# Retention and a SiLU MLP on one core: another order of the engines' work and of the loads from unit 3 to unit 9

## The chip, the cores and the metric

One Trainium2 chip, one of its cores. The metric is the device time of one launch in microseconds; the kernel is judged by the median of its runs. The engines that matter here are TensorE (PE), VectorE (DVE), ScalarE (ACT), GpSimd (POOL) and SyncE (SP), which issues the loads and stores. Each engine works through its own queue in program order; semaphores order the queues against each other.

## The reference

```python
# q, k, v: (B=4, H=8, S=768, D=64)
gamma = 1.0 - 2.0 ** (-5.0 - np.arange(H))
for t in range(S):
    state = gamma[None, :, None, None] * state + np.einsum('bhd,bhe->bhde', k[:, :, t], v[:, :, t])
    y[:, :, t] = scale * np.einsum('bhd,bhde->bhe', q[:, :, t], state)
...
x = y.transpose(0, 2, 1, 3).reshape(B * S, H * D)      # 3072 x 512
h = x @ w_in                                           # w_in: 512 x 2048
g = h * (1.0 / (1.0 + np.exp(-h)))
return g @ w_out                                       # w_out: 2048 x 512
```

A linear attention with a decay for each head, and a two-layer network with SiLU behind it. The weights come as float64 and are converted on the chip.

## The kernel before

**Tiling.** The 768 positions are cut into six chunks of 128. A unit is one chunk of one batch: unit n is chunk n // 4 of batch n % 4, 24 in all. Four units of one chunk make the 512 columns of one block `xt[c]`. The hidden layer has 16 slices of 128 features; a product (c, f) multiplies block c with slice f of w_in, goes through SiLU, and its result g is kept or stored. After all 96 products the output layer runs over the stored g. Each float32 operand is split into a rounded high part and a remainder, so a product has 12 matmuls of 512 columns: i = 0 and i = 1 (four each) sum up in `ha`, i = 2 in `hb`, and the three parts of x and of w are needed in that order.

**One unit.** Its steps have these names in the hand-written order of the first 60 us:

- T(n), `stage_t`: four transposes of k (tile `kp`) and four of q (`qp`) on PE (L482), each followed by a copy on ACT to `kt` and `qt` (L483). `kp` takes one of three PSUM banks in turn, `qp` has one bank.
- K(n), `scale_k`: k times its decay, one DVE instruction in place (L424). KA(n) does the same with eight small ACT instructions, one for each head (L932).
- SC(n): `stage_s`, 32 small matmuls that sum k times v (L510, needs the scaled k), and `stage_a`, 32 for the scores (L520). Both write the bank pair `s`, which is free when unit n-1 has been read out.
- A(n), three steps: DVE masks the scores (`am`, L528); `mid` (L534 on ACT in chunk 0, L536 on DVE later); DVE makes the next `state` (L540).
- Q(n), `scale_q`: q times its decay on DVE (L429), by `gq`, which `next_chunk` moves on by one chunk with four ACT instructions (L379).
- Y(n), `stage_y`: the masked scores times v (32 matmuls), the first half of the states times q, a fence through a one-element POOL memset (L406), and the second half (all L568), in the bank pair `y`. YA(n) is the first two, YB(n) the last.
- X(n), four steps: copy of y to SBUF on ACT (L615), rounding to the high part on ACT (`xh`, L639), the remainder on DVE ("lower", L642), and the third part on DVE ("third", L645).

**Beside the units.** W(i) is one slice of w_in in eleven steps, which convert it from float64 and split it (ACT L205, L212, L121, L127; DVE L208, L214, L218, L224, L124, L129). P(n) is product n (L740, c = n // 16, f = n % 16); `ha` and `hb` take two of the same three banks that `kp` uses, in turn. CL(n) closes it in three steps: copy of `ha` on ACT (L763), subtraction of `hb` on DVE (L768), SiLU on ACT (L773). Some filler matmuls with zeros (L317, L323) stand where PE would wait (`FILL_T` ahead of the transposes, `FILL_FENCE` inside Y, `FILL_P` ahead of a product).

**What sets the order.** PE's order is written out by hand throughout. SP, DVE, ACT and POOL follow the written order up to `early_order.close()`, just behind P(16); from there on a planner sets the order by its own costs and due times, with some places fixed by `issue_after`. Loads are written into SP's order by `load` and `load_w`; loads of units 8 and later rotate through three buffers for k, three for v and two for q; `hold(masked[0])` makes SP wait for the last mask before it goes on.

Of the kernel before, what the change touches and what calls it, by code (L numbers as in the profile page):

```python
# [34 lines left out]
def kernel(  # L35
# [35 lines left out]
    NF = DF // 128  # L71
# [69 lines left out]
    EARLY = 2 * B  # L141
# [32 lines left out]
    def load_w(i):  # L174
        if i >= 2 * NF:
            return
        if wide:
            t = stage.tile([128, 2 * DM], U32, tag="wf", name=f"wf_{i}")
            w_in, w_out, n = moe_w_in.bitcast(U32), moe_w_out.bitcast(U32), 256
        else:  # L180
            t = stage.tile([128, DM], FP32, tag="wf", name=f"wf_{i}")
            w_in, w_out, n = moe_w_in, moe_w_out, 128
        if i < NF:
            to = t.rearrange("p (i o f) -> o p i f", o=2, f=n)
            src = w_in[:, ts(i, n)].rearrange("(i o p) f -> o p i f", o=2, p=128)
            last[:] = [nc.sync.dma_start(out=to[0], in_=src[0]).ins]  # L186
            for j in range(2):
                nc.sync.dma_start(out=to[1, ts(j, D)], in_=src[1, ts(1 - j, D)])  # L188
        else:
            nc.sync.dma_start(out=t, in_=w_out[ts(i - NF, 128), :])  # L190
        staged[i] = t
# [128 lines left out]
    def narrow(out, n):  # L320

        for _ in range(n):
            nc.tensor.matmul(out[:, :32], lhsT=zero, rhs=zero[:, :32], start=True, stop=True,  # L323
                             skip_group_check=True)
# [52 lines left out]
    def next_chunk():  # L377
        for a in range(HP):
            nc.scalar.activation(out=gq[:, a, :], in_=gq[:, a, :], func=AF.Copy,  # L379
                                 scale=step[:, a : a + 1])  # L380
# [75 lines left out]
        nc.scalar.copy(out=to[n].bitcast(U16).rearrange("p a (t w) -> p w a t", w=2),  # L456
                       in_=turned.pop((name, n)).rearrange("p (w a) t -> p w a t", w=2))

    FILL_T = {2: (3, 2), 3: (0, 1)}
    NARROW_T = {0: (8, 5)}  # L460
    FILL_Y = {0: 1, 3: 4}
    NARROW_Y = {0: 8}
    idle = []
    FILL_FENCE = {0: 2, 2: 2, 3: 2}
    FILL_P = {(0, 0): 1, (1, 0): 2}

    def stage_t(n):

        src = kqv["k"][n], kqv["q"].pop(n)
        tp = turn(f"kp_{n}"), banks("q", f"qp_{n}", 1)[:, 0]  # L470

        def new(name, to, bufs):
            to[n] = one.tile([128, HP, C], FP32, tag=name, name=f"{name}_{n}", bufs=bufs)
            return to[n]

        made = ("kt", kt, 2), ("qt", qt, 3)
        if n not in ROWS:
            for i in range(2):
                fill(tp[i], FILL_T.get(n, (0, 0))[i])
                t = tp[i].rearrange("p (a t) -> p a t", a=HP)  # L480
                for a in range(HP):
                    nc.tensor.transpose(t[:, a, :], src[i][:, 2 * a : 2 * a + 2, :], ident)  # L482
                evac[:] = [nc.scalar.copy(out=new(*made[i]), in_=t).ins]  # L483
                if n in NARROW_T:
                    narrow(idle[0], NARROW_T[n][i])
            return
        tp = [t.rearrange("p (i a t) -> p i a t", i=2, a=HP) for t in tp]
        for i in range(2):
            for a in range(HP):
                for o in range(2):  # L490
                    nc.tensor.transpose(tp[o][:, i, a, :], src[i][ts(o, D), 2 * a : 2 * a + 2, :],  # L491
                                        ident[ts(o, D), ts(o, D)])
        made = [new(*m) for m in made]
        for o in range(2):
            for i in range(2):
                evac[:] = [nc.scalar.copy(out=made[i][:, :, ts(o, D)], in_=tp[o][:, i]).ins]
# [52 lines left out]
    def stage_y(n):  # L549

        vs, amn, qtn = kqv["v"].pop(n), am.pop(n), qt.pop(n)
        states = steps_of.pop(n)
        bank = banks("y", f"y_{n}")
        fill(bank[:, 0], FILL_Y.get(n, 0))
        narrow(bank[:, 0], NARROW_Y.get(n, 0))
        yp = bank[:, :, : 4 * D].rearrange("p o (a t) -> p o a t", a=HP)
        lone = None
        if n == len(units) - 1:
            lone = banks("s", f"yl_{n}")[:, :, : 4 * D].rearrange("p o (a t) -> p o a t", a=HP)

        started, done, new = set(), [], []

        def product(a, o, j, lhsT, rhs, apart_now=False):
            e = j ^ (a % 2)
            to = lone if apart_now else yp
            o = o ^ 1 if apart_now else o
            key = apart_now, e, o
            i = nc.tensor.matmul(to[ts(e, D), o, a, :], lhsT=lhsT, rhs=rhs,  # L568
                                 start=key not in started, stop=True,
                                 skip_group_check=True).ins  # L570
            started.add(key)
            if new:
                fence(done[-1], i)
                new.clear()
            done.append(i)

        def scores():
            for a in range(HP):
                for o in range(2):
                    for j in range(2):  # L580
                        product(a, o, j, vs[ts(o, D), 2 * a + j, :], amn[ts(o, D), j, a, :])

# [306 lines left out]
    YA(0), YB(0), X(0)  # L889
    T(1), K(1)  # L890
    W(0)
    load_w(2)
    W(0)
    X(0), X(0)
    SC(1), A(1)
# [8 lines left out]
    YB(1), X(1)  # L904
    A(2), Q(2), A(2)
    X(1)
    T(3), K(3)
    X(1), X(1)
    YA(2), YB(2), X(2)
    SC(3), A(3), A(3), Q(3), A(3)  # L910
    X(2), W(1), W(1)
    X(2), X(2)
    YA(3), YB(3), X(3), X(3)
    W(1), W(1)
    T(4)
    X(3), X(3)
    K(4)
    W(1), W(1)
    loads(EARLY - 2), loads(EARLY - 1)
    closing = {}  # L920

    def P(n):
        c, f = divmod(n, NF)
        closing[n] = close_steps(c, f, *multiply(c, f))

    def CL(f):
        next(closing[f], None)

    def KA(n):
        t = kqv["k"][n]  # L930
        for h in range(H):
            nc.scalar.activation(out=t[:, h, :], in_=t[:, h, :], func=AF.Copy,  # L932
                                 scale=gk[:, units[n][0], h : h + 1])

    P(0)
    next_chunk()
    SC(4)
    CL(0), CL(0), CL(0)
    put_g(0)
    W(1)  # L940
    T(5)
    A(4), A(4), Q(4), K(5), A(4)
    W(1), W(1)
    YA(4), SC(5), YB(4)
    loads(EARLY)
    W(2), W(1)
    A(5)
    W(1), W(2), W(2)
    X(4)
    T(6)  # L950
    P(1)
    A(5), Q(5), A(5)
    KA(6)
    W(2), W(2), W(2)
    load("k", EARLY + 1), load("q", EARLY + 1), load("v", EARLY + 1)
    W(2)
    CL(1), CL(1)
    W(2)
    YA(5), SC(6), YB(5)
    X(5)  # L960
    W(2), W(2)
    A(6)
    W(2)
    CL(1)
    put_g(0)
    T(7)
    P(2)
    K(7), A(6), Q(6), A(6)
    X(4), X(5), X(4), X(4)
    CL(2)  # L970
    YA(6), SC(7), YB(6)
    X(6)
    T(8)
    A(7)
    hold(masked[0])
    load("k", EARLY + 2), load("q", EARLY + 2)
    load_w(3)
    load("v", EARLY + 2)
    load_w(4)
    A(7), Q(7)  # L980
    next_chunk()
    K(8), A(7)
    CL(2), CL(2)
    put_g(0)
    X(5), X(5)
    X(6)
    YA(7), SC(8), YB(7)
    X(7), X(7)
    A(8)
    X(6), X(6)  # L990
    T(9)
    load("k", EARLY + 3), load("q", EARLY + 3)
    X(7), X(7)
    A(8), Q(8), A(8)
    P(NF)
    KA(9)
    CL(NF), CL(NF)
    taken[0] = 3
    begin_w()
    CL(NF)  # L1000
# [194 lines left out]
```

## Time and profile before

| | |
|---|---|
| runs | 611.75, 612.47, 614.08 us, median 612.47 |
| profiled execution | 611.64 us, span 609.5 us |
| granted TensorE clock | 1.00 throughout |
| HBM traffic | 66.06 MB read, 36.70 MB written |
| written order ends (end of P(16)) | about 55.2 us into the span |

The span runs from the first to the last instruction of the profile. Views of the trace used in this document: busy time by stretches, timelines of one engine, the waits (who waited for whom), and the loads with their time to landing. Times in them are from the start of the span; an end of a matmul is modelled, the starts are recorded. Behind 56 us PE runs without a wait that the view of waits names.

### The profile page before, as it was taken

The numbers are of one execution on the slowest core, as the hardware profiler recorded it, in microseconds if no ns is written. First come the engines' busy times: TensorE is split into PE (matmuls) and PEld (weight loads), VectorE is DVE, ScalarE is ACT, GpSimd is POOL, SyncE is SP. The second block draws the span as 40 slices with busy tenths as digits, with TensorE's granted clock in tenths as the row PEclk, the third lists the DMA queues.
The fourth block names the chain that finished last, engine by engine and source line by source line (L and its number), as shares of the span: only waits on it lengthen the run. The fifth ranks groups of instructions, "written<-read, shape, count | busy, mean of one in ns | idle before, by whom it ended". The sixth has DMA issues, their size and how long they took to land.

```text
span 609.5 us, 13714 instructions
## 1 busy us (share of the span) xinstructions
PE 600.8 (99%) x5509; PEld 495.8 (81%) x5509; DVE 396.3 (65%) x673; ACT 325.0 (53%) x599; POOL 33.3 (5%) x89
## 2 busy tenths in 40 slices
PE   8999999999999999999999999999999999999997
PEld 6787788888888888888888888888888888888886
DVE  4888998678876766766699765535454553645532
ACT  7788777678776677666789622221221412313111
POOL 3000110100031112110000000000000000000000
PEclk9999999999999999999999999999999999999999
DMA  9998787776799699999777433524423342533201
GB/s 195 215 213 194 190 224 250 238 238 203 252 246 209 173 271 270 246 265 283 258 266 239 157 122 100 176 69 127 151 100 109 138 129 79 171 105 112 96 1 69
DMA packets 144335, 108.90 MB, mean 179 GB/s; under 512 B 101136, under 2 KB 109584, under 8 KB 144272
## 3 DMA queue, kind: packets, MB, share of 16 engines
q1 hardware_dynamic: 144272, 108.03, 62.7%
q8 instruction: 43, 0.70, 0.5%
q14 instruction: 20, 0.16, 0.1%
HBM read 66.06 MB, written 36.70 MB: 169 GB/s over the span
## 4 chain that ended last, share of the span: by engine, by line
PE 93%; SPq 4%; DVE 2%; DMA 1%; ACT 0%; issue 0%; DVEq 0%
PE ha L740 29%; PE o L1117 21%; PE hb L740 14%; PE oa L1117 14%; PE ob L1117 7%; PE y L568 3%; SPq L166 3%; PE sc L510 1%; PE sc L520 1%; DMA kqv<-in_q_dram 1%; PE o L1137 0%; SPq L188 0%; PE kp L482 0%; SPq L186 0%; PE kp L491 0%
## 5 line engine op out<-in xcount | busy, mean ns | idle before, releaser
L740 PE MATMUL ha<-xt,wi 128*128 128x512 f32 x768 | 193.0, 393 | 0.4 <-DVE xt L642 0.3
L740 PEld LDWEIGHTS ha<-xt,wi 128*128 128x128 f32 x768 | 142.4, 188 | 31.4 <-DVE xt L642 0.8
L1117 PE MATMUL o<-wo,gs 128*128 128x512 f32 x564 | 143.1, 389 | 0.0
L828 ACT ACTIVATE gs<-gr 128x512 fp32r<-128x512 f32 x96 | 53.2, 621 | 139.0 <-issue 138.0
L1117 PEld LDWEIGHTS o<-wo,gs 128*128 128x128 f32 x564 | 105.9, 188 | 22.0
L830 DVE TENSOR_TENSOR gs<-gr,gs 128x512 fp32r<-128x512 f32 x96 | 62.1, 684 | 94.2 <-ACT gs L828 94.2
L1117 PE MATMUL oa<-wo,gs 128*128 128x512 f32 x376 | 115.7, 389 | 0.0
L740 PE MATMUL hb<-xt,wi 128*128 128x512 f32 x384 | 102.6, 389 | 0.0
L768 DVE TENSOR_TENSOR g<-g,hb 128x512 f32<-128x512 f32 x87 | 59.5, 684 | 53.8 <-ACT g L763 41.2
L740 PEld LDWEIGHTS hb<-xt,wi 128*128 128x128 f32 x384 | 72.1, 188 | 15.1
L1117 PEld LDWEIGHTS oa<-wo,gs 128*128 128x128 f32 x376 | 70.5, 188 | 14.6
L1117 PE MATMUL ob<-wo,gs 128*128 128x512 f32 x188 | 73.1, 389 | 0.0
L773 ACT ACTIVATE g<-g 128x512 f32<-128x512 f32 x87 | 54.7, 628 | 33.3 <-DVE g L768 33.1
L763 ACT ACTIVATE g<-ha 128x512 f32<-128x512 f32 x87 | 51.7, 594 | 27.0 <-PE ha L740 18.1
L831 DVE SCALAR_TENSOR_TENSOR gs<-gs 128x512 fp32r<-128x512 f32 x96 | 62.0, 683 | 0.1
L1117 PEld LDWEIGHTS ob<-wo,gs 128*128 128x128 f32 x188 | 35.3, 188 | 7.3
L205 ACT ACTIVATE ca<-wf 128x512 f32<-128x512 f32 x32 | 21.6, 674 | 7.2 <-DVE cs L218 3.1
L1158 ACT ACTIVATE o<-o 128x512 f32<-128x512 f32 x10 | 6.0, 600 | 33.4 <-PE o L1117 33.0
L218 DVE SCALAR_TENSOR_TENSOR cs<-ca,cs 128x512 uint32<-128x512 uint32 x32 | 23.2, 725 | 0.9
L528 DVE TENSOR_TENSOR am<-sc,decay 128x512 f32<-128x512 f32 x24 | 16.5, 688 | 10.3 <-PE sc L520 10.2
L645 DVE SCALAR_TENSOR_TENSOR xt<-xt 128x512 fp32r<-128x512 f32 x28 | 20.1, 724 | 0.7
L568 PE MATMUL y<-qt,mid 64*64 64x64 f32 x376 | 19.4, 219 | 0.3 <-issue 0.3
(132 smaller groups left out, 580.6 us busy)
## 6 DMA issues: line engine op xcount, KB each, us to landing
gr<-gd SPq DMA_DIRECT2D x96, 256.0 KB, 2.7
gd<-g SPq DMA_DIRECT2D x87, 256.0 KB, 3.5
wf<-in_moe_w_out_dram SPq DMA_DIRECT2D x16, 512.0 KB, 4.8
out_dram<-o SPq DMA_DIRECT2D x23, 256.0 KB, 2.1
wf<-in_moe_w_in_dram SPq DMA_DIRECT2D x16, 256.0 KB, 4.1
wf<-in_moe_w_in_dram SPq DMA_DIRECT2D x32, 128.0 KB, 4.1
kf<-in_k_dram SPq DMA_DIRECT2D x16, 256.0 KB, 4.5
qf<-in_q_dram SPq DMA_DIRECT2D x16, 256.0 KB, 4.3
```

Of the source, the lines that this page charges most:

```text
L205: top = nc.scalar.activation(out=a.bitcast(FP32), in_=hi.bitcast(FP32), func=AF.Abs, scale=2.0 ** -3).ins
L218: nc.vector.scalar_tensor_tensor(out=s, in0=a, scalar=3, in1=s, op0=ALU.logical_shift_left, op1=ALU.bitwise_xor)
L568: i = nc.tensor.matmul(to[ts(e, D), o, a, :], lhsT=lhsT, rhs=rhs, start=key not in started, stop=True, skip_group_check=True).ins
L645: nc.vector.scalar_tensor_tensor(out=x[2], in0=x[1].bitcast(FP32), scalar=-1.0 / EPS, in1=x[0].bitcast(FP32), op0=ALU.mult, op1=ALU.add)
L740: nc.tensor.matmul(hb if i == 2 else ha, lhsT=w_sb[f][:, i, ts(kk, 128)], rhs=xt[c][:, i, kk, :], start=kk == 0 and i != 1, stop=kk == KIN ...
L763: copied[:] = [nc.scalar.activation(out=hs, in_=ha, func=AF.Copy, scale=ONE_E).ins]
L768: taken_out[:] = [nc.vector.tensor_tensor(out=hs, in0=hs, in1=hb, op=ALU.subtract).ins]
L773: nc.scalar.activation(out=hs, in_=hs, func=AF.Silu)
L828: nc.scalar.activation(out=t[:, 0, :], in_=g, func=AF.Copy, scale=HALF)
L830: nc.vector.tensor_tensor(out=t[:, 1, :], in0=g, in1=high, op=ALU.subtract)
L831: nc.vector.scalar_tensor_tensor(out=t[:, 2, :], in0=t[:, 1, :].bitcast(FP32), scalar=-1.0 / EPS, in1=high, op0=ALU.mult, op1=ALU.add)
L1117: nc.tensor.matmul(o, lhsT=g, rhs=wo[f][:, i, :], start=f == 0 and i != 1, stop=f == NF - 1 and i != 0 or (b, f, i) == (B - 1, early_f - 1 ...
```

## The change

The part of the written order from T(3) to P(16) is replaced by another one, with the same steps. Single pieces that differ: T(n) and YA(n) can be called in halves (TK and TQ, YS and Y0), so that a unit's k and q transposes can stand apart; two fillers are taken out (`FILL_T` of unit 3, `FILL_FENCE` of unit 2); unit 7's k is scaled by KA on ACT and not by K on DVE; both halves of Y(7) stand ahead of SC(8) on PE; the k half of T(6) stands ahead of SC(5), and the q half behind YB(4); CL(0) stands behind both halves of T(5); `next_chunk` stands ahead of unit 3's copy of y and, the second time, ahead of CL(2)'s SiLU. On SP, the third slice of w_in goes out behind unit 6's q, unit 9's v ahead of unit 8's, and unit 10's k and the fourth slice ahead of the hold. The products are each issued whole, as before.

```diff
-    FILL_T = {2: (3, 2), 3: (0, 1)}
+    FILL_T = {2: (3, 2)}
...
-    FILL_FENCE = {0: 2, 2: 2, 3: 2}
+    FILL_FENCE = {0: 2, 3: 2}
...
     def stage_t(n):
+        list(steps_t(n))
+
+    def steps_t(n):
...
                 if n in NARROW_T:
                     narrow(idle[0], NARROW_T[n][i])
+                yield
             return
...
+    tsteps = {}
+
+    def TK(n):
+        tsteps[n] = steps_t(n)
+        next(tsteps[n])
+
+    def TQ(n):
+        next(tsteps[n])
+
     def YA(n):
+        YS(n), Y0(n)
+
+    def YS(n):
         ys[n] = stage_y(n)
         ys[n][0]()
+
+    def Y0(n):
         ys[n][1](0)
...
-    load_w(2)
...
-    T(3), K(3)
-    X(1), X(1)
-    YA(2), YB(2), X(2)
-    SC(3), A(3), A(3), Q(3), A(3)
-    X(2), W(1), W(1)
-    X(2), X(2)
-    YA(3), YB(3), X(3), X(3)
-    W(1), W(1)
-    T(4)
-    X(3), X(3)
-    K(4)
-    W(1), W(1)
-    loads(EARLY - 2), loads(EARLY - 1)
...
-    P(0)
-    next_chunk()
-    SC(4)
-    CL(0), CL(0), CL(0)
-    put_g(0)
-    W(1)
-    T(5)
-    A(4), A(4), Q(4), K(5), A(4)
-    W(1), W(1)
-    YA(4), SC(5), YB(4)
-    loads(EARLY)
-    W(2), W(1)
-    A(5)
-    W(1), W(2), W(2)
-    X(4)
-    T(6)
-    P(1)
-    A(5), Q(5), A(5)
-    KA(6)
-    W(2), W(2), W(2)
-    load("k", EARLY + 1), load("q", EARLY + 1), load("v", EARLY + 1)
-    W(2)
-    CL(1), CL(1)
-    W(2)
-    YA(5), SC(6), YB(5)
-    X(5)
-    W(2), W(2)
-    A(6)
-    W(2)
-    CL(1)
-    put_g(0)
-    T(7)
-    P(2)
-    K(7), A(6), Q(6), A(6)
-    X(4), X(5), X(4), X(4)
-    CL(2)
-    YA(6), SC(7), YB(6)
-    X(6)
-    T(8)
-    A(7)
-    hold(masked[0])
-    load("k", EARLY + 2), load("q", EARLY + 2)
-    load_w(3)
-    load("v", EARLY + 2)
-    load_w(4)
-    A(7), Q(7)
-    next_chunk()
-    K(8), A(7)
-    CL(2), CL(2)
-    put_g(0)
-    X(5), X(5)
-    X(6)
-    YA(7), SC(8), YB(7)
-    X(7), X(7)
-    A(8)
-    X(6), X(6)
-    T(9)
-    load("k", EARLY + 3), load("q", EARLY + 3)
-    X(7), X(7)
-    A(8), Q(8), A(8)
-    P(NF)
-    KA(9)
-    CL(NF), CL(NF)
```

In the diff above the old order stands whole. The new order, which the full diff has one call to a line, here with several to a line and nothing left out:

```python
TK(3) X(1) load("k",6) YS(2) TQ(3) Y0(2) K(3) X(1) YB(2) X(2) X(2) SC(3) A(3) A(3) W(1) Q(3)
load("q",6) load_w(2) YS(3) X(2) load("k",7) next_chunk() A(3) Y0(3) YB(3) W(1) X(3) X(3)
load("v",6) TK(4) load("q",7) TQ(4) X(2) W(1) load("v",7) W(1) W(1) W(1) X(3) X(3)
load("v",9) K(4) W(1) P(0) SC(4) A(4) A(4) W(1) Q(4) TK(5) A(4) TQ(5) K(5) load("q",8)
YS(4) CL(0) W(1) Y0(4) TK(6) SC(5) CL(0) YB(4) W(1) Q(5) CL(0) X(4) A(5) W(1) W(2) W(2)
load("k",8) A(5) A(5) TQ(6) W(2) KA(6) W(2) P(1) load("q",9) load("k",9) W(2) W(2)
YS(5) CL(1) Y0(5) put_g(0) SC(6) W(2) CL(1) Q(6) load("v",8) W(2) W(2) A(6) YB(5) X(4)
W(2) A(6) X(5) load_w(3) W(2) TK(7) TQ(7) CL(1) X(4) A(6) P(2) load("k",10) KA(7) X(4)
YS(6) CL(2) X(5) Y0(6) put_g(0) SC(7) YB(6) X(6) CL(2) TK(8) TQ(8) A(7) Q(7) A(7) YS(7)
K(8) Y0(7) next_chunk() X(5) CL(2) YB(7) hold(masked[0]) A(7) X(7) X(5) X(6) X(6) X(7)
TK(9) SC(8) X(7) load("v",10) load_w(4) load("q",10) A(8) load("k",11) TQ(9) put_g(0)
A(8) X(7) KA(9) X(6) P(NF) load("q",11) Q(8) CL(NF) A(8) CL(NF)
```

More of the change, by code (lines that the diff above doesn't have):

```diff
@@ L933, in KA @@
                                  scale=gk[:, units[n][0], h : h + 1])
+    TK(3)
+    X(1)
+    load("k",6)
+    YS(2)
+    TQ(3)
+    Y0(2)
+    K(3)
+    X(1)
+    YB(2)
+    X(2)
+    X(2)
+    SC(3)
+    A(3)
+    A(3)
+    W(1)
+    Q(3)
+    load("q",6)
+    load_w(2)
+    YS(3)
+    X(2)
+    load("k",7)
+    next_chunk()
+    A(3)
+    Y0(3)
+    YB(3)
+    W(1)
+    X(3)
+    X(3)
+    load("v",6)
+    TK(4)
+    load("q",7)
+    TQ(4)
+    X(2)
+    W(1)
+    load("v",7)
+    W(1)
+    W(1)
@@ L935 @@
+    W(1)
+    X(3)
+    X(3)
+    load("v",9)
+    K(4)
+    W(1)
     P(0)
-    next_chunk()
     SC(4)
-    CL(0), CL(0), CL(0)
-    put_g(0)
-    W(1)
-    T(5)
-    A(4), A(4), Q(4), K(5), A(4)
-    W(1), W(1)
-    YA(4), SC(5), YB(4)
-    loads(EARLY)
-    W(2), W(1)
-    A(5)
-    W(1), W(2), W(2)
-    X(4)
-    T(6)
-    P(1)
-    A(5), Q(5), A(5)
-    KA(6)
-    W(2), W(2), W(2)
-    load("k", EARLY + 1), load("q", EARLY + 1), load("v", EARLY + 1)
-    W(2)
-    CL(1), CL(1)
-    W(2)
-    YA(5), SC(6), YB(5)
@@ L960 @@
-    X(5)
-    W(2), W(2)
-    A(6)
+    A(4)
+    A(4)
+    W(1)
+    Q(4)
+    TK(5)
+    A(4)
+    TQ(5)
+    K(5)
+    load("q",8)
+    YS(4)
+    CL(0)
+    W(1)
+    Y0(4)
+    TK(6)
+    SC(5)
+    CL(0)
+    YB(4)
+    W(1)
+    Q(5)
+    CL(0)
+    X(4)
+    A(5)
+    W(1)
+    W(2)
+    W(2)
+    load("k",8)
+    A(5)
+    A(5)
+    TQ(6)
+    W(2)
+    KA(6)
+    W(2)
+    P(1)
+    load("q",9)
+    load("k",9)
+    W(2)
+    W(2)
+    YS(5)
+    CL(1)
+    Y0(5)
+    put_g(0)
+    SC(6)
@@ L963 @@
     W(2)
     CL(1)
+    Q(6)
+    load("v",8)
+    W(2)
+    W(2)
+    A(6)
+    YB(5)
+    X(4)
+    W(2)
+    A(6)
+    X(5)
+    load_w(3)
+    W(2)
+    TK(7)
+    TQ(7)
+    CL(1)
+    X(4)
+    A(6)
+    P(2)
+    load("k",10)
+    KA(7)
+    X(4)
+    YS(6)
+    CL(2)
+    X(5)
+    Y0(6)
     put_g(0)
-    T(7)
-    P(2)
-    K(7), A(6), Q(6), A(6)
-    X(4), X(5), X(4), X(4)
+    SC(7)
+    YB(6)
+    X(6)
     CL(2)
-    YA(6), SC(7), YB(6)
-    X(6)
-    T(8)
-    A(7)
-    hold(masked[0])
@@ L976 @@
-    load("k", EARLY + 2), load("q", EARLY + 2)
-    load_w(3)
-    load("v", EARLY + 2)
+    TK(8)
+    TQ(8)
+    A(7)
+    Q(7)
+    A(7)
+    YS(7)
+    K(8)
+    Y0(7)
+    next_chunk()
+    X(5)
+    CL(2)
+    YB(7)
+    hold(masked[0])
+    A(7)
+    X(7)
+    X(5)
+    X(6)
+    X(6)
+    X(7)
+    TK(9)
+    SC(8)
+    X(7)
+    load("v",10)
     load_w(4)
-    A(7), Q(7)
-    next_chunk()
-    K(8), A(7)
-    CL(2), CL(2)
+    load("q",10)
+    A(8)
+    load("k",11)
+    TQ(9)
     put_g(0)
-    X(5), X(5)
@@ L986 @@
-    X(6)
-    YA(7), SC(8), YB(7)
-    X(7), X(7)
-    A(8)
-    X(6), X(6)
-    T(9)
-    load("k", EARLY + 3), load("q", EARLY + 3)
-    X(7), X(7)
-    A(8), Q(8), A(8)
-    P(NF)
-    KA(9)
-    CL(NF), CL(NF)
+    A(8)
+    X(7)
+    KA(9)
+    X(6)
+    P(NF)
+    load("q",11)
+    Q(8)
+    CL(NF)
+    A(8)
+    CL(NF)
     taken[0] = 3
```

## The prediction

> **What bounds the kernel now.** The page first: the span, then TensorE's share of it.
>
> ```profile
> span 609.5 us, 13714 instructions
> ...
> PE 600.8 (99%) x5509; PEld 495.8 (81%) x5509; DVE 396.3 (65%) x673; ACT 325.0 (53%) x599; POOL 33.3 (5%) x89
> ```
>
> TensorE is busy for 600.8 of 609.5 us, so a reordering can earn only what it takes out of 8.7 us of idle time, and of filler matmuls. Next, busy time by stretch, for the part that the change touches (17.90 us, the transposes of unit 3, to 55.19, the end of P(16)), with one stretch behind it. After the stretch and its length come busy time (and count) of PE, PEld, DVE, ACT, POOL, then the granted clock, the DMA share and GB/s.
>
> ```profile
> 17.90:29.32 11.42, 10.72 (x201) 7.86 (x199) 9.32 (x17) 8.93 (x19) 0.18 (x2) 1.00 0.97 225
> 29.32:35.51 6.19, 5.44 (x210) 4.90 (x209) 5.31 (x10) 4.42 (x9) 0.09 (x1) 1.00 1.01 201
> 35.51:41.31 5.80, 5.80 (x152) 4.96 (x150) 5.56 (x12) 4.73 (x15) 0.09 (x1) 1.00 0.89 192
> 41.31:46.27 4.96, 4.96 (x143) 4.11 (x141) 3.83 (x8) 3.44 (x7) 0.09 (x1) 1.00 0.97 213
> 46.27:55.19 8.92, 8.05 (x165) 6.30 (x159) 8.80 (x16) 8.46 (x22) 0.09 (x1) 1.00 0.79 191
> 70.00:85.00 15.00, 15.00 (x319) 12.43 (x318) 14.23 (x25) 11.86 (x24) 3.44 (x5) 1.00 0.76 173
> ```
>
> In the first five rows, which together are the part that changes, PE is busy 34.97 of 37.29 us: 2.32 us are idle. The two fillers that go (below) are 0.77 us of the busy time. So about 3.1 us is all that the new order can save, even if it closes every gap. Against that, DVE is busy 32.82 of 37.29 us and ACT 29.98: neither has room for a wait of its own followed by a burst. From 55 us on the view of waits shows none for PE, so a shift at 55.19 reaches the end whole.
>
> Third, PE's timeline, in order of time (start, duration, line, tile; in brackets idle time and what ended it).
>
> ```profile
> 18.40 0.38 PE L317 MATMUL qp<-zero 128*128 128x512 bf16 x1
> 20.03 0.39 PE L317 MATMUL y<-zero 128*128 128x256 bf16 x2
> 26.29 2.19 PE L740 MATMUL ha<-xt,wi 128*128 128x512 f32 x8
> 29.32 0.69 PE L510 MATMUL sc<-kqv 64*64 64x64 f32 x32
> 30.41 0.66 PE L482 MATMUL kp<-ident,kqv 128*128 128x128 f32 x4
> 30.90 0.60 PE L482 MATMUL qp<-ident,kqv 128*128 128x128 f32 x4
> 31.43 0.69 PE L568 MATMUL y<-am,kqv 64*64 64x64 f32 x32
> 32.35 0.27 PE L568 MATMUL y<-qt,state 64*64 64x64 f32 x1 [0.23 <-DVE qt L429]
> 33.33 0.69 PE L510 MATMUL sc<-kqv 64*64 64x64 f32 x32 [0.52 <-PE y L568]
> 35.51 2.09 PE L740 MATMUL ha<-xt,wi 128*128 128x512 f32 x8
> 38.44 0.69 PE L568 MATMUL y<-am,kqv 64*64 64x64 f32 x32
> 39.18 0.65 PE L510 MATMUL sc<-kqv 64*64 64x64 f32 x32
> 39.65 0.65 PE L520 MATMUL sc<-qt,kt 64*64 64x64 f32 x32
> 41.31 2.09 PE L740 MATMUL ha<-xt,wi 128*128 128x512 f32 x8
> 45.00 0.65 PE L510 MATMUL sc<-kqv 64*64 64x64 f32 x32
> 53.23 1.20 PE L740 MATMUL ha<-xt,wi 128*128 128x512 f32 x4 [0.34 <-DVE xt L642]
> 55.19 1.99 PE L740 MATMUL ha<-xt,wi 128*128 128x512 f32 x8
> ```
>
> PE's prices are distances between starts: half a transpose stage 0.5 us (30.41, 30.90, 31.43), a product 2.93 (35.51 to 38.44), the Y scores with the first half of the states 0.74 (38.44 to 39.18), the sums of a unit 0.47, and as many score matmuls again. The second half of the states takes about 0.35.
>
> Fourth, ACT and DVE in the same way. A distance is what an instruction costs its queue; its duration is when the result is there.
>
> ```profile
> 23.05 0.37 ACT L534 COPY mid<-sc 128x256 f32<-128x256 f32 x1 [1.11 <-DVE am L528]
> 31.10 0.59 ACT L483 COPY kt<-kp 128x512 f32<-128x512 f32 x1 [0.27 <-PE kp L482]
> 31.58 0.59 ACT L483 COPY qt<-qp 128x512 f32<-128x512 f32 x1
> 32.06 0.64 ACT L121 ACTIVATE wi<-cs 128x512 fp32r<-128x512 f32 x1
> 32.59 0.66 ACT L205 ACTIVATE ca<-wf 128x512 f32<-128x512 f32 x1
> 36.40 2.02 ACT L932 ACTIVATE kqv<-kqv,gk 128x64 f32<-128x64 f32 x8
> 38.33 0.58 ACT L763 ACTIVATE gk<-ha 128x512 f32<-128x512 f32 x1
> 47.93 1.28 ACT L379 ACTIVATE gq<-gq,step 128x128 f32<-128x128 f32 x4
> 41.72 0.68 DVE L424 TENSOR_TENSOR kqv<-kqv,gk 128x512 f32<-128x512 f32 x1
> 42.32 0.41 DVE L536 TENSOR_TENSOR mid<-state,sc 128x256 f32<-128x256 f32 x1
> 42.65 0.68 DVE L429 TENSOR_TENSOR qt<-qt,gq 128x512 f32<-128x512 f32 x1
> ```
>
> An ACT copy costs 0.48 (31.10, 31.58, 32.06), an ACTIVATE of 512 columns 0.53 (32.06, 32.59), that of L205 or L212 some 0.57, the eight scalings of KA 1.93 (36.40 to 38.33), next_chunk 1.2. A DVE instruction costs 0.60 over 512 columns (41.72 to 42.32) and 0.33 over 256. A consumer on another engine starts about 0.05 after the producer's end.
>
> **The change, part by part.** Two fillers go: one matmul ahead of unit 3's q transposes and two behind unit 2's first states (0.38 and 0.39 us). Both lie in waits: the first before Y(2), which needs its mask, the second in the fence, which PE must sit out anyway. I take 0 for them, between 0 and -0.77.
>
> Up to P(0) the work is the same with next_chunk drawn ahead of unit 3's copy of y. The copy of mid(3) stands at 23.05; L205 (0.57) and next_chunk (1.2) behind it leave ACT free at about 25.05. P(0) needs the copy that follows and the rounding behind it, 0.61 + 0.64 later: 26.3, and it started at 26.29. So this stage gives 0 (between -0.2 and +0.3), and the sums of unit 4 start at 29.32 again.
>
> Stage two, to P(1). PE: sums and scores to 30.41, both halves of T(5) to 31.43, then Y(4)'s scores, and its states, which need Q(4) on DVE as at 32.35. Next in line is now TK(6). Its bank was that of P(0)'s first half, which CL(0) empties on ACT, and CL(0) now stands behind both copies of T(5): 31.10 + 2 x 0.48 = 32.06, done at 32.64. TK(6) runs 32.7 to 33.2, in the hole that ended at 33.33. The sums of unit 5 need K(5), by DVE's queue (mask 30.6, mid, Q, state, K) done at 33.15, so they start at 33.2; scores, second states and TQ(6) follow, and P(1) starts at 33.2 + 0.5 + 0.47 + 0.35 + 0.46 = 34.98, not 35.51: -0.53.
>
> Stage three, to P(2). P(1) ends at 37.9, Y(5) at 38.65. The sums of unit 6 need KA(6). ACT's order ahead of it: copy for TK(6) at 33.39, L127 33.87, silu 34.39, copy of y(4) 34.92, L205 35.4, copy for TQ(6) 35.97, L212 36.45, so KA(6) runs 37.03 to 39.05. It was done at 38.42 before. PE stands 0.4 us for it, and the sums start at 39.05 to 39.1, against 39.18. P(2) then starts at 41.1: -0.2 is left.
>
> Stage four holds the largest term. K(7), one DVE instruction of 0.60, becomes KA(7), 1.93 on ACT, and stands behind eight others that follow KA(6). They are: CL(1) 38.96, L121 39.48, rounding of x(4) 40.0, then L127, whose operand comes from DVE: subtraction 39.58 (it needs CL(1)'s copy), Q(6) 40.18, L124 40.78, done 41.47. So ACT stands from 40.5 to 41.5, then: L127 41.5, copy of y(5) 42.03, both copies of T(7) 42.5 and 42.97, silu 43.44, KA(7) 43.97 to 45.99. P(2) waits at most 0.2 us for the same L127 (42.15) and ends at 44.05, Y(6) at 44.8, and the sums of unit 7 stand until 45.99, where they started at 45.00. If the sums wait head by head, they end at 46.2, if for the whole tile, at 46.5; I take 46.35, and the scores of unit 7 end at 46.8. They ended at 45.00 + 2 x 0.47 = 45.94: from -0.2 to +0.9, a loss of 1.1.
>
> Stage five. CL(2)'s copy follows KA(7), done 46.5, and DVE goes on in order: subtraction 46.53, mask(7) 47.13, Q 47.73, mid 48.33, K(8) 48.67, lower(5) 49.27, state(7) 49.87, third(5) 50.2, and, behind ACT's copies, next_chunk, silu and roundings (xh6 done at 51.56), lower(6) 51.6, lower(7) 52.2, mask(8) 52.8, mid 53.4, third(7) 53.73, third(6) 54.33, done 55.02. P(16) can start at 52.2 behind TQ(9) and its fillers, but its last four matmuls need third(6): they run 55.06 to 55.97. P(16) ended at 55.19: +0.8. That Y(7) now stands ahead of the scores of unit 8 costs nothing beside this: state(7) ends 50.29 and holds those either way.
>
> Loads: SP's stream has the same transfers in another order, k6 and q6 in the place of the third w_in slice, v9 ahead of v8.
>
> ```profile
> 26.15 0.66 SPq L186 DMA_DIRECT2D wf<-in_moe_w_in_dram  x1
> 31.99 1.01 SPq L166 DMA_DIRECT2D kqv<-in_k_dram  x1
> DMA to landing us min/median/max: 3.2/5.0/5.9
> ```
>
> With 5.9 us at most, k6 is there by 32.1 for TK(6) at 32.7, v6 (now in the slot of 31.99) by 37.9 for 39.1. The hold now has v10, the fifth slice, q10, k11 and q11 behind it, but k10 and the fourth slice ahead. v11 will wait for unit 9's v buffer, not unit 8's; it is used long after. I take 0 for all of this; without the 0.6 us that k6 has to spare, each later us costs one.
>
> **The sum.** 0 - 0.53 + 0.33 + 1.1 - 0.1 = +0.8 us at 55.97, and behind it 0, since ACT and DVE stand to PE as before. On the profiled execution, 611.64 us, this is 612.4; on the median 612.47, 613.3. A few hundredths in each of some forty queue steps make it good to about 1 us each way, 612.3 to 614.3, if one of the cases below does not take its place.
>
> **The rivals.** Gain: ACT does not hold unit 7's sums. It speaks for it that ACT's only stand, 1.0 us, hangs on one DVE step (L124 behind Q(6)). Without it KA(7) ends at 45.0 and everything behind it comes 1.0 sooner; if next_chunk's 1.2 us on ACT then no longer stand ahead of lower(6) either, because the roundings find ACT free, the end of P(16) is another 1.2 us sooner: 0.8 - 1.0 - 1.2 = -1.4, 611.1. Against it: all of ACT's steps from 33.39 on are back to back.
>
> Loads pace the stage: the DMA share is 0.97 to 1.01 up to 35.5 us, so that no order helps and none hurts: 612.5. Against it: the only waits in the PE rows from 29 us on name DVE and PE.
>
> Slower: the queues behind 56 us, which follow a planner's times, come out in another order. Between 70 and 85 us DVE is busy 14.23 of 15. A product's bank comes free with a DVE subtraction; each put one instruction further back costs 0.60 once PE has no bank left. From five such places it decides: 0.8 + 5 x 0.6 = +3.8, 616.3.
>
> Clock: PE's idle rises from 0.75 in the 6.19 us from 29.32 (clock 1.00) to about 1.2 in the 3.3 us from TQ(9) at 51.75 to 55.06. Were the clock to halve there, the next product would take twice 2.93: +0.8 + 2.9, 616.2. The Trainium skill, "TensorE: Matmul & The Clock Gate", section "A second HAM failure mode: psum-queue depth-cycling", tells of short idles between groups that make the clock oscillate; that speaks against fewer fillers, though this trace holds 1.00 through each of its waits.
>
> **How the numbers follow.** Forecast 0.62, gain 0.15 (0.03 of it beyond 0.5%, which asks for all of the 3.1 us), loads 0.07, later queues 0.12, clock 0.04. About 0.5%, 3.1 us, is what a measurement of this kernel tells from no change. So faster 0.03, same 0.82, slower 0.15 (the last two, less what stays under 615.5). The time is 613.3; the range from the gain rival to just short of the slower ones, 610.8 to 616.0.
>
> **What would show it.** Right: unit 7's sums at about 46.0 with a wait for L932, the eight small ACTIVATEs, P(1) at 35.0, the last four matmuls of P(16) at 55.1 behind DVE's third, PE without waits from 56 on. Wrong: KA(7) done by 45, P(16) over before 55, a load named in a PE wait, or gaps in PE between 60 and 110 us.

## The result and the profile after

The changed kernel takes 614.18 us (median of 21 runs, 613.03 to 618.27) beside 612.42 us (21 runs) of the kernel before: a ratio of 1.0032, 95% interval 1.002 to 1.0044, or 2.0 us (1.2 to 2.7). It is slower, by less than 0.5%. The sign and the place of the forecast's largest term are right; the size, +0.8 us, is too small.

The page of the changed kernel: the span, TensorE's share, and the queue that brings PE's own program (packets, MB, share). Below it the first stretch (after the stretch and its length: busy time and count of PE, PEld, DVE, ACT, POOL, then clock, DMA share, GB/s).

```profile
span 615.9 us, 13713 instructions
PE 605.3 (98%) x5506; PEld 498.9 (81%) x5506; DVE 397.0 (64%) x672; ACT 325.9 (53%) x607; POOL 33.6 (5%) x89
...
q8 instruction: 43, 0.70, 0.5%
```

```profile
0.00:21.75 21.75, 18.15 (x421) 14.36 (x421) 9.66 (x19) 13.22 (x37) 5.18 (x43) 0.84 0.94 201
```

T(3) starts at 21.75 us here, not at 17.91: this one execution (618.05 us) lost 3.8 us ahead of T(3), at a mean clock of 0.84, around a wait of 1.60 us for unit 1's v. The old order can lose it too: before_w3 (below) waits the same 1.60 us and starts T(3) at 20.56. The stages are therefore read from a second profile of the same kernel, after_again (615.77 us, span 613.7), in which T(3) starts at 17.93, so that its times can be laid beside the prediction's without a shift. Its stretches, cut at the same events as the prediction's:

```profile
17.93:29.22 11.29, 10.42 (x198) 7.67 (x196) 9.89 (x19) 8.86 (x19) 0.18 (x2) 1.00 1.06 217
29.22:34.95 5.73, 5.59 (x209) 4.84 (x209) 4.26 (x8) 3.46 (x8) 0.09 (x1) 1.00 0.78 189
34.95:41.12 6.17, 6.17 (x151) 5.23 (x150) 5.55 (x12) 5.68 (x16) 0.09 (x1) 1.00 1.03 212
41.12:47.22 6.10, 6.02 (x143) 4.62 (x142) 4.11 (x8) 5.51 (x15) 0.09 (x1) 1.00 0.94 198
47.22:57.29 10.07, 8.21 (x164) 6.71 (x159) 8.30 (x16) 8.30 (x23) 0.09 (x1) 1.00 0.89 213
72.10:87.10 15.00, 15.00 (x320) 12.39 (x319) 14.24 (x25) 11.89 (x24) 3.44 (x5) 1.00 0.82 184
```

The same five stages took 11.42, 6.19, 5.80, 4.96 and 8.92 us before. The second is 0.46 shorter, the third 0.37, the fourth 1.14 and the fifth 1.15 longer. From T(3) to the start of P(17) that is 39.36 us instead of 37.28.

ACT, DVE and PE of the same profile where the fourth and fifth stages lose their time:

```profile
44.18 2.02 ACT L936 ACTIVATE kqv<-kqv,gk 128x64 f32<-128x64 f32 x8
46.09 0.59 ACT L767 ACTIVATE gk<-ha 128x512 f32<-128x512 f32 x1
```

```profile
46.71 0.69 DVE L772 TENSOR_TENSOR gk<-gk,hb 128x512 f32<-128x512 f32 x1 [1.99 <-ACT gk L767]
47.32 0.68 DVE L532 TENSOR_TENSOR am<-sc,decay 128x512 f32<-128x512 f32 x1
...
51.71 1.29 DVE L646 TENSOR_TENSOR xt<-ys,xt 128x512 fp32r<-128x512 f32 x2 [0.64 <-ACT xt L643]
53.73 0.69 DVE L532 TENSOR_TENSOR am<-sc,decay 128x512 f32<-128x512 f32 x1 [0.73 <-PE sc L524]
...
54.67 1.29 DVE L649 SCALAR_TENSOR_TENSOR xt<-xt 128x512 fp32r<-128x512 f32 x2
```

```profile
34.95 2.09 PE L744 MATMUL ha<-xt,wi 128*128 128x512 f32 x8
...
41.12 2.46 PE L744 MATMUL ha<-xt,wi 128*128 128x512 f32 x8
...
45.18 1.35 PE L514 MATMUL sc<-kqv 64*64 64x64 f32 x29
...
51.22 0.41 PE L524 MATMUL sc<-qt,kt 64*64 64x64 f32 x16
53.20 0.46 PE L524 MATMUL sc<-qt,kt 64*64 64x64 f32 x16 [1.57 <-issue]
```

KA(7) runs 44.18 to 46.20, and the 29 sums that PE has ready at 45.18 spread over 1.35 us, until KA(7) has released the last head. CL(2)'s copy stands behind KA(7), and DVE waits 1.99 us for it. All this is as forecast. The last line is not: after half of unit 8's scores PE stands 1.57 us, and no engine is named for it. DVE, ready for mask(8) at about 53.0, waits for those scores.

### The profile page after: what moved, and what is told of

It is laid out like the page before. It is cut to its first block, busy times and chain, and to the rows that moved or that the text cites. A ratio compares the mean times of both kernels' runs of the same rounds, so it can differ in the third digit from the quotient of the medians.

```text
span 615.9 us, 13713 instructions
## 1 busy us (share of the span) xinstructions
PE 605.3 (98%) x5506; PEld 498.9 (81%) x5506; DVE 397.0 (64%) x672; ACT 325.9 (53%) x607; POOL 33.6 (5%) x89
## 4 chain that ended last, share of the span: by engine, by line
PE 92%; ACT 2%; DMA 2%; DVE 1%; issue 1%; SPq 1%; POOL 0%; ACTq 0%; DVEq 0%; POOLq 0%
PE ha L744 27%; PE o L1216 21%; PE oa L1216 14%; PE hb L744 13%; PE ob L1216 7%; PE y L572 4%; PE sc L514 2%; PE sc L524 2%; DMA kqv<-in_v_dram 1%; DMA yr<-yd 1%; PE kp L485 1%; SPq L166 1%; PE qp L485 0%; PE o L1236 0%; ACT xt L643 0%
## 5 line engine op out<-in xcount | busy, mean ns | idle before, releaser
L649 DVE SCALAR_TENSOR_TENSOR xt<-xt 128x512 fp32r<-128x512 f32 x28 | 22.1, 799 | 0.5
```

What stands on the lines that cost most here:

```text
L649: nc.vector.scalar_tensor_tensor(out=x[2], in0=x[1].bitcast(FP32), scalar=-1.0 / EPS, in1=x[0].bitcast(FP32), op0=ALU.mult, op1=ALU.add)
```

## The experiments

Ratios are against the kernel before, run beside each kernel on the same chip. "S(n)" is the start of unit n's sums; stretches are in us. A stand is idle time of PE that the profile puts down to no engine ("issue").

| kernel | T(3) to S(4) | S(4) to T(8) | T(8) to P(17) | P(17) to the end | stand inside Y(6) | stand inside A(8) or Y(7) | ratio |
|---|---|---|---|---|---|---|---|
| before | 11.41 | 16.95 | 8.92 | 554.31 | none | none | |
| before_again | 11.87 | 17.05 | 9.42 | 554.27 | none | 1.02 | 1.0 (0.9973 to 1.0028) |
| before_w3 | 11.61 | 16.98 | 12.53 | 554.32 | none | 2.67 | 1.0012 (0.9987 to 1.0037) |
| after | 11.85 | 18.02 | 9.30 | 554.98 | none | 1.08 | 1.0032 (1.002 to 1.0044) |
| after_again | 11.29 | 18.00 | 10.07 | 556.41 | none | 1.57 | 1.005 (1.003 to 1.007) |
| old_start | 12.38 | 17.75 | 9.01 | 554.75 | none | none | 1.0035 (1.001 to 1.0059) |
| hold_all | 11.24 | 17.75 | 9.56 | 555.27 | none | 1.08 | 1.0046 (1.0029 to 1.0064) |
| after_loads | 14.08 | 17.76 | 9.00 | 557.38 | none | 0.42 | 1.0027 (0.9996 to 1.0057) |
| after_quiet | 13.55 | 17.76 | 9.00 | 557.79 | none | none | 1.0064 (1.0038 to 1.009) |
| third_first | 11.87 | 18.73 | 8.74 | 554.50 | 0.64 | 0.53 | 1.0022 (1.0002 to 1.0042) |
| k7_dve | 11.54 | 17.70 | 9.04 | 555.14 | 0.38 | 0.80 | 1.0017 (0.9993 to 1.004) |
| k7_hold | 11.46 | 16.98 | 9.01 | 555.96 | none | none | 1.002 (1.0 to 1.0039) |
| k7_hold_third | 11.28 | 17.69 | 8.48 | 555.71 | 0.37 | 0.25 | 1.0028 (1.001 to 1.0046) |
| k7_quiet | 11.26 | 17.75 | 9.00 | 556.15 | 0.44 | none | 1.0053 (1.003 to 1.0077) |

**after_again**, the changed kernel once more.

> The changed kernel, not edited, for an execution with an ordinary start (in the profile of after, unit 1's v landed late, 1.6 us of PE wait at 12.2 to 13.8, ahead of everything that the change touches). Theory A (written order: stage one costs 0.4, KA(7) on ACT costs 1.5 by the start of T(8), P(16) ends 1.5 to 1.9 later than before, counted from the start of T(3)): from T(3)'s first transpose to the first of T(8)'s 29.9 us as in the profile of after (28.36 before), P(16)'s end 1.5 to 1.9 us later than before, time 1.003 of before. Theory B (the loss is an accident of the start or of the clock, and the order costs what the prediction said): T(3) to T(8) 29.2 or less, P(16)'s end at most 1.0 later than before. Theory C (PE's own stall of 1.08 us inside A(8), put down to issue, sets the end of P(16)): that stall is there again, at the same place.

Its stages are read above. From T(3) to P(17) it is 2.08 us longer than before, which is more than theory A's 1.5 to 1.9 and far from theory B. The stand is there again at the same place, as theory C expects.

**k7_dve.** Is it KA(7) on ACT?

```diff
-    KA(7)
+    K(7)
```

> Unit 7's k is scaled by one DVE instruction at the place in the order where KA(7) stood. Theory A: the sums of unit 7 no longer stand for ACT, T(3) to T(8) falls from 29.9 to about 29.0 us, ACT's copy for CL(2) and with it DVE's subtraction and mask(7) come 1.0 to 1.9 sooner, P(16) ends 1.0 to 1.4 sooner than in the changed kernel: 1.000 to 1.0015 of before. Rival (DVE is the bound, and 0.60 us more on it takes the place of the wait): T(3) to T(8) falls, P(16) ends within 0.3 of the changed kernel: 1.003. Theory C: P(16)'s end is set by PE's stall in A(8): gain under 0.5 us, 1.0025.

PE in k7_dve (T(3) starts 0.47 us later than before, at 18.38):

```profile
45.64 0.65 PE L514 MATMUL sc<-kqv 64*64 64x64 f32 x32
46.10 0.65 PE L524 MATMUL sc<-qt,kt 64*64 64x64 f32 x32
47.37 0.33 PE L572 MATMUL y<-qt,mid 64*64 64x64 f32 x2 [0.38 <-issue]
```

The sums of unit 7 run closed up again, in 0.46 us (45.64 to 46.10) where they took 1.2 with KA(7), so KA(7) did hold them. P(17) starts 38.28 us behind T(3), 1.08 sooner than in after_again, but 1.03 of that lies behind T(8), where this profile's stand is 0.80 us and not 1.57. S(4) to T(8) is 17.70, hardly less than the 17.75 of other profiles with KA(7): right behind the scores of unit 7 PE now stands 0.38 us without a named engine. The ratio, 1.0017 beside 1.005 in the same comparison, has an interval that overlaps the other. What KA(7) costs is therefore read below, from a pair without that stand.

**third_first.** Are the third parts of x, last in DVE's queue, what holds P(16)?

```diff
     load("q",10)
+    X(7)
+    X(6)
     A(8)
...
     A(8)
-    X(7)
     KA(9)
-    X(6)
     P(NF)
```

> DVE does the third parts of units 7 and 6 ahead of mask(8) and mid(8). Prediction's stage five: P(16)'s last four matmuls no longer wait for third(6), its end comes 0.4 to 0.9 us sooner: 1.002 of before. Theory C: PE reaches P(16) too late for third(6) to matter, gain 0 to 0.1: 1.003. Mask(8), 1.2 us later, may hold Y(8) behind P(17): no, since that has over 3 us to spare.

The last stage is 8.74 us instead of 9.00 to 10.07, with a stand of 0.53 inside; but a second stand of 0.64 in Y(6) had come ahead of it, and P(17) starts 39.34 behind T(3), as in after_again. The thirds bind only where PE has not stood. That is seen in k7_hold, below, where PE waits 0.65 us for one.

**old_start.** Does the new order up to P(0), with its two fillers fewer, cost anything? T(3) to P(0) goes back to the old sequence, the fillers come back.

```diff
-    FILL_T = {2: (3, 2)}
+    FILL_T = {2: (3, 2), 3: (0, 1)}
-    FILL_FENCE = {0: 2, 3: 2}
+    FILL_FENCE = {0: 2, 2: 2, 3: 2}
...
+    T(3), K(3)
+    X(1), X(1)
+    YA(2), YB(2), X(2)
+    SC(3), A(3), A(3), Q(3), A(3)
...
```

> From T(3) to just ahead of P(0) the order of before on PE, ACT and DVE, with its two fillers, next_chunk behind K(4); the loads stay as in the changed kernel and the rest of the order too. Theory A: T(3) to S(4) falls from 11.85 us to 11.4 (as before), and the end of P(16) comes 0.4 sooner: 1.0025. The prediction's stage one: no difference, 1.003. If the missing fillers cost clock: clocks of 1.000 in all runs and a gain above 0.4.

A miss: 12.38 us to S(4), with a stand of 1.27 us inside without a named engine, against 11.29 in after_again. So this run doesn't price the old start; the new one shows no loss against the 11.41 us of before (11.24 in hold_all, which has no stand there). Behind S(4) the profile has none: S(4) to P(17) is 26.76 us.

**hold_all, k7_hold, k7_hold_third, before_w3.** The stand could be PE's own program arriving late, because unit 10's k and the fourth w_in slice now go out ahead of the hold. hold_all puts both behind it; k7_hold adds K(7) on DVE, k7_hold_third the thirds ahead as well; before_w3 puts k10 and the slice ahead of the hold in the kernel before.

```diff
# hold_all
-    load("k",10)
...
-    load_w(3)
...
     hold(masked[0])
+    load("k",10)
+    load_w(3)
# before_w3
+    load("k", EARLY + 2)
+    load_w(3)
     hold(masked[0])
-    load("k", EARLY + 2), load("q", EARLY + 2)
-    load_w(3)
+    load("q", EARLY + 2)
...
```

> The changed kernel with unit 10's k and the fourth w_in slice back behind the hold on SP, as before; nothing else moves. Theory F (PE stands inside A(8) because the next block of its own instructions is fetched late, behind the loads that the new order put ahead of the hold; a quiet queue at 46 to 48 us let it through in the kernel before): the stall of 0.5 to 1.6 us put down to issue inside A(8) shrinks to 0.3 or less, P(16) then waits for third(6), and its end, counted from T(3), goes from 39.2 to 39.4 down to about 38.5: ratio 1.002. Rival G (the stall sits at a fixed count of PE instructions and has nothing to do with the loads): it stays at 0.5 to 1.6 us, no gain.

> Unit 7's k scaled on DVE, and unit 10's k and the fourth slice behind the hold. With K(7) on DVE alone the end of P(16), counted from T(3), was 38.28 with 0.8 us of stall in A(8). Theory F with theory A (KA(7) holds the sums of unit 7): the two gains add, no such stall, 37.4 to 37.7, as in the kernel before (37.28): ratio 1.000. Rival G: 38.3, 1.0015.

> As k7_hold, with the third parts of units 7 and 6 ahead of mask(8). If third(6) is what PE waits for once the stall is gone: another 0.3 to 0.6 us, 37.0 from T(3) to the end of P(16), 0.9995 of before. If PE's own work is the bound by then: no difference from k7_hold.

> The kernel before with one thing of the change alone: unit 10's k and the fourth w_in slice go ahead of the hold. Theory F: a stall put down to issue appears in PE between 48 and 52 us, 0.5 to 1.5 us long, and the end of P(16) moves by 0 to 0.9 us (P(16) waits until 53.2 for x anyway, so part of it is covered): 1.000 to 1.0015 of before. Rival G: no new stall, no difference; the third w_in slice... is not touched by this.

One row of PE's timeline in before_w3, then two in k7_hold:

```profile
55.55 0.27 PE L568 MATMUL y<-qt,state 64*64 64x64 f32 x1 [2.67 <-issue]
```

```profile
55.90 1.20 PE L744 MATMUL hb<-xt,wi 128*128 128x512 f32 x4 [0.65 <-DVE xt L649]
60.57 0.27 PE L495 MATMUL kp<-ident,qf 64*128 64x64 f32 x1 [0.35 <-DMA qf<-in_q_dram]
```

Two results for the theory, two against it: before_w3 got a stand of 2.67 us and k7_hold has none, but hold_all keeps 1.08, and before_w3's ratio of 1.0012 over its runs says that 2.67 us is not what it usually pays. The place of these two loads alone does not decide it.

The pair hold_all and k7_hold differs in KA(7) alone and has no stand ahead of T(8): S(4) to T(8) falls from 17.75 to 16.98 (before 16.95). So KA(7) costs 0.8 us there. But in the three other kernels with K(7) on DVE (k7_dve, k7_hold_third, k7_quiet) the stretch stays at 17.69 to 17.75: PE comes sooner to Y(6) and stands there 0.37 to 0.44 us, and some 0.6 us pass between the starts of the two matmuls around the stand. Of the seven profiles with KA(7) only third_first has that stand. The two waits overlap, and without KA(7) PE gains its 0.8 us only where Y(6) has no stand.

From T(3) to P(17) k7_hold takes 37.45 us, as expected; its ratio is over the expected 1.000, and in its profile 1.6 us more than before pass behind P(17). S(4) to P(17) is 25.99 (25.87 before), so even with K(7) on DVE the new order gains nothing by the end of P(16): PE waits 0.65 us for the third. It waits 0.46 and 0.47 us for it with KA(7) too (old_start, after_quiet); how much of the 0.65 is K(7)'s was not separated. k7_hold_third, with the thirds ahead, has no such wait, and its last stage is 8.48 us, 0.53 less than k7_hold and 0.44 less than before. Its whole is a miss all the same, 37.45 us to P(17) for an expected 37.0 and a ratio of 1.0028: the stands in Y(6) and A(8) take the gain.

**after_quiet, k7_quiet, after_loads, before_again.** The same question from other sides: SP held a second time, so that nothing loads while PE is in A(8), with KA(7) and without; all loads in their old order; and the kernel before once more.

```diff
# after_quiet, k7_quiet
-    load("v",10)
-    load_w(4)
-    load("q",10)
     A(8)
+    hold(masked[0])
+    load("v",10)
+    load_w(4)
+    load("q",10)
     load("k",11)
# after_loads, two of its places
...
+    load("k", 6), load("q", 6), load("v", 6), load("k", 7), load("q", 7), load("v", 7)
     P(0)
...
     hold(masked[0])
+    load("k", 10), load("q", 10)
+    load_w(3)
+    load("v", 10)
+    load_w(4)
...
```

> The changed kernel with SP held a second time, on unit 8's mask, ahead of v10, the fifth w_in slice and q10: between the fourth slice and the mask at about 53.7 us no load is queued. If TensorE's stand inside unit 8's scores (1.57 us in the repeat, with no engine named) is its own program arriving late behind loads, it is under 0.4 us here, the end of P(16), counted from unit 3's transposes, falls from 39.36 to about 38.3 (KA(7) is left) and the ratio from 1.005 to about 1.003. If it doesn't hang on loads: a stand of 0.5 us or more stays there, and the end is over 39.

> The same with K(7) on VectorE: both causes out. If they are the whole loss ahead of P(16): its end at 37.3 to 37.6 (before 37.28; 38.28 with K(7) alone), and the ratio 1.000 to 1.0015, what is left being waits behind P(16). If the load order does more than that: over 38.

> The changed kernel's order of all engines, with SP's loads in the order of the kernel before (third slice early, k10 to the fifth slice behind the hold). If the loss lies in the engines' order (KA(7) on ScalarE): end of P(16) at 38.2 or more from unit 3's transposes and a ratio of 1.002 to 1.005. If the load order makes it: end at about 37.3 and a ratio within 0.001 of 1.

> The kernel before, unchanged, for a second profile. If TensorE's stands without a named engine were luck of one profile, one of over 0.5 us shows up between unit 3's transposes and the end of P(16) here too, and that end differs from 37.28 by over 0.5 us; if they belong to the order of the loads, all are under 0.5 us and the end is 37.3 to 37.6. Ratio 1.

The last stage in after_quiet, T(8) to P(17), and two rows of its PE timeline; then one row of before_again:

```profile
50.81:59.81 9.00, 8.25 (x164) 6.54 (x159) 8.20 (x16) 8.85 (x24) 0.09 (x1) 1.00 0.17 41
```

```profile
58.78 1.19 PE L744 MATMUL hb<-xt,wi 128*128 128x512 f32 x4 [0.47 <-DVE xt L649]
...
64.45 0.27 PE L495 MATMUL kp<-ident,qf 64*128 64x64 f32 x1 [1.36 <-DMA qf<-in_q_dram]
```

```profile
51.76 0.27 PE L568 MATMUL y<-qt,state 64*64 64x64 f32 x1 [1.02 <-issue]
```

With the DMA share down to 0.17 there is no stand inside A(8), in either quiet kernel. But the expected gain of the whole is a miss, 1.0064 and 1.0053: for one thing, unit 10's q now comes late and PE waits 1.36 and 1.50 us for it. In k7_quiet P(17) also starts 38.01 us behind T(3), not 37.3 to 37.6, with the stand in Y(6). after_loads settles what the loads' order is worth: with the old one, S(4) to T(8) is 17.76 and S(4) to P(17) 26.76, just as in old_start and after_quiet. So these 0.89 us up to P(16) belong to the engines' order. And before_again has a stand of 1.02 us too, in its Y(7): such stands are no property of the new order.

What they are: the trace's transfer records have the 43 blocks of 16 KB that queue q8 brings PE. Between T(3) and P(17) the 14 profiles have 23 stands, and two things hold for every one. First, the place: each is ahead of the 476th, 603rd, 1111th or 1237th matmul of the program, in order of their starts, in the old kernel as in the new (in A(8) or Y(7) it is always the 1237th). These are 127, four times 127 and 126 matmuls apart, or, with a weight load for each matmul, some 254 instructions to a block. Second, the time: each ended 1.31 to 1.76 us after the block of that place had landed, for the stand of 2.67 us in before_w3 as for the 0.25 us in k7_hold_third. Where PE comes later than that it passes without a stand: the 1237th matmul starts 2.60 us after the landing in k7_hold and 1.85 in before. Nowhere up to there does PE go on with a block sooner than 1.31 us after its landing. This shows the stands to be waits for PE's program: rival G has the place right, theory F the late block.

How late a block lands changes from run to run: the one for the 1237th matmul landed 3.51 us behind the one before it in k7_hold, 4.48 in before, 6.76 in after_again and 6.89 in before_w3. That other loads make it late would fit the quiet kernels (4.52 and 4.26), but hold_all (5.58) shows that no single move avoids it, and how often a run pays for it stays open. The Trainium skill, "Runtime: NRT & Kernel Launch", section "Instruction fetch mechanics", has it that the sequencer fetches 16 KiB blocks of 256 instructions by a DMA queue of its own and that this is mostly hidden. The block size agrees with the records; hidden it is not at these 23 places.

**Behind P(16).** The three profiles of the kernel before take 554.27 to 554.32 us from P(17) on, the new order 554.50 to 557.79, though the order of every queue behind P(16) is the same. One place shows how. ACT, DVE and POOL of before around the third parts of block 2, whose y comes back from HBM (`yr`):

```profile
164.06 0.63 ACT L639 ACTIVATE xt<-yr 128x512 fp32r<-128x512 f32 x1 [0.67 <-DMA yr<-yd]
```

```profile
166.42 1.29 DVE L645 SCALAR_TENSOR_TENSOR xt<-xt 128x512 fp32r<-128x512 f32 x2
...
167.22 1.39 POOL L438 COPY kp<-kf 128x1024 uint16<-128x1024 uint16 x1 [0.19 <-DVE xt L645]
```

The same in after_again, where P(17) starts 2.10 us later, and PE behind it:

```profile
167.08 0.63 ACT L643 ACTIVATE xt<-yr 128x512 fp32r<-128x512 f32 x1 [1.03 <-DMA yr<-yd]
```

```profile
168.83 0.69 DVE L646 TENSOR_TENSOR xt<-yr,xt 128x512 fp32r<-128x512 f32 x1 [0.39 <-ACT xt L643]
169.44 2.97 DVE L649 SCALAR_TENSOR_TENSOR xt<-xt 128x512 fp32r<-128x512 f32 x2
...
169.27 1.16 POOL L438 COPY kp<-kf 128x1024 uint16<-128x1024 uint16 x1 [0.18 <-POOL token L406]
170.37 1.50 POOL L438 COPY qp<-qf 128x1024 uint16<-128x1024 uint16 x1
```

```profile
172.56 1.16 PE L744 MATMUL hb<-xt,wi 128*128 128x512 f32 x4 [0.51 <-DVE xt L649]
```

Counted from P(17), y is rounded at 108.87 us before and at 109.79 here: the reload landed later. DVE's two thirds, begun at 111.23 before, begin at 112.15, and POOL's copies begin at 112.03 and 111.98. Before, the second third (166.42 + 0.60 = 167.02) had begun when POOL's copy came; here each copy was there first, and the pair takes 2.97 us, not 1.29. PE waits 0.51 us for it. Over all profiles the pair takes 1.29 (before, before_w3), 2.12 to 2.13 (before_again and seven others) or 2.97, and PE waits for it only where it is 2.97: in after (0.46), after_again (0.51), k7_hold_third (0.43) and after_loads (0.88).

In after that place is nearly all that the tail loses. In after_again, laid beside before matmul by matmul from P(17) on, PE loses time at three places: 0.7 us here, then 0.4 and 0.8 us at two products at about 201 and 205 us, where it waits 0.15 and 0.52 us for ACT's copies of `ha`. The first of these copies stands for a store of g (`gd`), before and in after_again:

```profile
196.49 0.60 ACT L763 ACTIVATE g<-ha 128x512 f32<-128x512 f32 x1 [1.06 <-DMA gd<-g]
```

```profile
200.82 0.60 ACT L767 ACTIVATE g<-ha 128x512 f32<-128x512 f32 x1 [2.58 <-DMA gd<-g]
```

Why the reload and the store land later was not settled.

No version that was run is faster than the kernel before.

## Why the prediction was right or wrong

**Stage one, 0: right.** 11.29 us against 11.41, and 11.24 to 11.87 in seven more profiles of this order; where it is more (13.55 and 14.08) a stand without a named engine and a clock of 0.87 to 0.88 were in it.

**Stages two and three: right to 0.2 us.** P(1) was put at 34.98 and starts at 34.95; P(2) at 41.1, it starts at 41.12. ACT's queue, counted by its distances, gave KA(6) 37.03 to 39.05; it runs 37.25 to 39.26.

**Stage four, +1.1: right.** KA(7) was put at 43.97 to 45.99 and runs 0.2 later; the second half of Y(6), next in PE's queue, starts at 46.79, where the scores were to end at 46.8. In four other profiles with KA(7) (old_start, hold_all, after_loads, after_quiet) S(4) to T(8) is 17.75 or 17.76, 0.8 over before, against 1.05 in after_again. That KA(7) makes it, the pair hold_all and k7_hold shows: 17.75 and 16.98. (The three other profiles with K(7) keep some 17.7, with the stand in Y(6) in its place.)

**Stage five, P(16) over at 55.97: the first step that failed.** DVE's times hold as far as lower(7): the subtraction 46.71 for 46.53, mask(7) 47.32 for 47.13, the remainders 51.71 for 51.6. Then mask(8) comes at 53.73, not 52.8, since the scores it reads are not there: PE itself stood. The step took it that PE has what it executes, and PE stood for its own program. Where the stand is absent or covered (old_start, after_quiet, after_loads), S(4) to P(17) is 26.76 us, 0.89 over before, for a forecast of 0.8, and in the first two the wait for the third is there, 0.46 and 0.47 us. With it the stretch is 27.32 (after), 27.31 (hold_all) or 28.07 (after_again). The kernel before can pay the same: 26.47 in before_again. The trace of before had shown two such stands, 0.27 and 0.43 us, in its waits, and the forecast gave them no price.

**Behind P(16), 0: the second step that failed.** ACT and DVE do not "stand to PE as before": DVE's thirds hang on a reload, ACT's copies of `ha` on a store, and DVE was only 0.2 us ahead of POOL at one place (167.02 against 167.22). The price is 0.7 and 2.1 us in the two profiles of the changed kernel (0.2 to 3.1 in the experiments that do not wait for q10). With the 0.89 up to P(16) that makes 1.6 to 3.0 us; the runs give 1.2 to 2.7. The measured time lies in the range of 610.8 to 616.0, but that range was drawn between rivals that did not come about (below), so it is partly luck: the sum behind 613.3 has less than half of the 2.0 us.

**The loads, 0:** right from S(4) to P(16) (after_loads). Behind it unit 10's q, which now goes out behind unit 10's v and the fifth slice, landed 6.6 us ahead of its first use before and 2.4 us in after_again; in k7_dve, k7_hold and k7_hold_third it came late and PE waited 0.18 to 0.35 us for it.

**The rivals.** Gain: its condition, ACT free of KA(7), was made in k7_hold, and P(16) ended 0.12 us behind the kernel before, not 1.4 ahead: the 1.4 us are not there, and PE waits for DVE's third instead. Loads pace the stage: false, the old order of loads leaves the 0.89 us in place (after_loads). Later queues in another order: false, they are the same; but what it put a price on, DVE and ACT giving PE's operands and banks late, is how the tail lost its time. Clock: 1.00 in every stretch of after_again, through a stand of 1.57 us, so the rival did not come about there.

## What to carry to other kernels

Counting a queue by its distances gives the new times to 0.2 us, as long as the engine has its instructions and its data; where small instructions run dense, look in the waits for stands with no engine named, and give them a price in both kernels. A saving can also vanish where a second wait lies under the first: with KA(7) gone, the late program block took its place in three of four kernels. An operation moved to the engine with more idle time can still be dear: ask what stands behind it in that queue (here the copy that frees DVE's next four steps), not how busy the engine is. Behind the change, "the same order" is not "the same time": look for places where two engines miss each other by a few tenths of a microsecond.

## What the hardware showed

DVE's two-operand instruction over 512 columns takes 0.69 us, and about 1.5 beside a POOL copy: the pair needs 1.29 alone and 2.97 with both under the copies. The Trainium skill, "SBUF — State Buffer", section "SBUF: two separate sides", says that VectorE with two SBUF inputs and GpSimd share one pair of ports and that whichever starts first keeps it for its whole instruction; both orders of before and after_again agree with that.

PE's stands for its program were 0.15 to 2.67 us, 23 in all, in every kernel but one of the table at least once between T(3) and P(17). And one of 2.67 us, in before_w3, leaves the clock below 1:

```profile
49.15:61.68 12.53, 9.39 (x164) 7.83 (x159) 8.89 (x16) 8.83 (x23) 0.09 (x1) 0.86 0.76 185
```

The mean of 0.86 over this stretch is what the prediction's clock rival had in mind; the stand's length alone does not tell when it comes. after_again's 1.57 us left the clock at 1.00, while stage one has a mean of 0.87 in after_quiet and 0.88 in after_loads, with stands of 0.82 and 1.08 us in it. What else it takes was not settled.
